# Narrowing the moving operand of a mixture's matmuls from 256 to 224 columns, and splitting a queue of twelve scatters into pairs

## The chip, the cores and the metric

The kernel runs on one core of a Trainium2 chip. The metric is the device time of one execution in microseconds (us); the kernel before takes 814.52 us, the median of three runs (814.19 to 816.84).

## The reference, cut to what matters

Three layers follow one another on 1536 tokens of 512 features. A retention layer makes the tokens. The first mixture sends each token to the one of eight experts that its gate prefers; each expert takes at most `capacity` = 384 tokens, in token order. The second mixture runs all tokens through four experts and adds them up, weighted by `domain_probs`.

```python
expert_idx = np.argmax(x @ w_gate, axis=1)
...
for i in range(N):                      # N = 1536, E = 8, capacity = N // E * 2 = 384
    e = expert_idx[i]
    if counts[e] < capacity:
        disp[e, counts[e]] = x[i]; pos[i] = counts[e]; counts[e] += 1; keep[i] = True
h = np.maximum(np.einsum('ecd,edf->ecf', disp, w1), 0.0)    # D = 512 -> F = 1024
y = np.einsum('ecf,efd->ecd', h, w2)
...
for e in range(4):                      # second mixture, all tokens
    out += p[:, e:e + 1] * (np.maximum(x @ w1[e], 0.0) @ w2[e])
```

With the reference's default inputs the gate gives the eight experts 183, 196, 188, 167, 213, 180, 203 and 206 tokens.

## The kernel before

The work runs in stages, one behind another on TensorE (PE). The order of every engine is that of the code; tile pools and semaphores add the waits.

Retention and routing come first (up to 91 us). Each of 12 blocks of 128 tokens is computed, written to a table in DRAM (`xd`), and its gate, its expert and its rank within the expert are worked out. From these come `gidx` (for each expert and each of `SL` = 256 slots the row of `xd` that sits there; an empty slot points at a row of zeros), `offi` (the column at which an expert's tokens begin in the sorted order) and `nbi` (whether any expert has more tokens than slots). If one has, the branch in `overflow()` (L566 to L654) runs the surplus in blocks of 128; otherwise it is jumped over.

The first mixture is the loop over `e` (L785 to L830). Numbers are split into a high part rounded to the matmul type fp32r and a rest, and each product is three fp32r matmuls (`PASS`). An expert has 8 weight chunks of 512 KB, which SP loads into `raw` tiles (4 buffers), ACT copies to the high part (L105) and DVE subtracts to the rest (L106), six chunks ahead (`split_w`, `DEPTH`). Per expert:

- m1 (L795): 4 groups of 24 matmuls, 128x128 weights, 256 moving columns (`x[:, sx, k]`, the slots). Two halves (`ff`) share one PSUM bank of 512 columns. Each group is evacuated by ACT (relu, L779) and DVE (rest, L780) over 512 columns.
- `prep_x(e + 1)` (L669): 8 transposes turn the next expert's gathered rows around, ACT and DVE copy them (L683, L684), and POOL gathers the rows of expert `e + 3` (L556, two indirect DMAs).
- for `e` = 0 `tables()` (L717): DVE and ACT compute for each token its four output weights (`tt`) and its place in the sorted order (`posi`). POOL then issues 12 scatters (L768) that write `tt` to the DRAM table `td`, one behind another since all write the same tile, and reads the table back as `tl` (L772). `tl` is first used by the second mixture's evacuations (L873).
- m2 (L817): 2 groups of 48 matmuls with 256 moving columns, each evacuated to the sorted columns `ds(ra, SL)` of `x2h` (ACT, L825) and `x2l` (DVE, L826). An expert's unused slots lie over the next expert's columns and are overwritten by it.

The second mixture (L836 to L891) does the same with 512 moving columns: n1 (L846) and n2 (L867), 24 stages of 96 matmuls. The tail scatters the rows to the output.

Where the trace names an F32 matmul (L297, L307, L338, L488) one call of the program is two instructions; an fp32r matmul (L795, L817, L846, L867) is one.

Of the kernel before, what the change touches and what calls it, by code (L numbers as in the profile page):

```python
# [8 lines left out]
F32 = mybir.dt.float32  # L9
# [10 lines left out]
P = 128  # L20
# [7 lines left out]
KF = F // P  # L28
XW = KD * 136
SL = 256  # L30
FMAX = 3.4028234663852886e38
PASS = ((0, 0), (0, 1), (1, 0))
WARM0 = 11
# [9 lines left out]


def blocks_of(cap):
    return max(SL // P, -(-min(cap, N) // P))


@with_exitstack
def tile_retention_moe_moe(ctx: ExitStack, tc, qkv, cst, gqt, a1, a2, b1, b2, dp, out, cap):  # L50
    nc = tc.nc
    NB = blocks_of(cap)
    drops = cap < N
    general = NB > SL // P

    pc = ctx.enter_context(tc.tile_pool(name="pc", bufs=1))
    pd = ctx.enter_context(tc.tile_pool(name="pd", bufs=1, space=DRAM))
# [82 lines left out]
    with ExitStack() as actx:  # L140
# [378 lines left out]
        nc.vector.tensor_tensor(out=cnt[:, 1], in0=cps, in1=cnt[:, 0], op=ALU.subtract)  # L519
        if general:  # L520
            nc.vector.tensor_scalar(
                out=nbf, in0=cnt[:, 0], scalar1=float(SL), scalar2=None, op0=ALU.is_gt
            )
            for j in range(3, NB):
                nc.vector.scalar_tensor_tensor(
                    out=nbf, in0=cnt[:, 0], scalar=float(j * P), in1=nbf,
                    op0=ALU.is_gt, op1=ALU.add,
                )
            nc.vector.tensor_copy(nbi[:, 0:8], nbf)
            nc.vector.tensor_reduce(out=nbi[:, 8:9], in_=nbf, axis=AX.X, op=ALU.max)  # L530
# [35 lines left out]
    def overflow():  # L566
        some = nc.values_load(nbi[0:1, 8:9], min_val=0, max_val=NB)
        with tc.If(some > 0), tc.tile_pool(name="pg", bufs=1, side="right") as pg:
            clear_x2()
            nx = NB - SL // P  # L570
            gi = pg.tile([P, nx, E1], I32, name="gi")
            rkm = pg.tile([P, NT], F32, name="rkm")
            nc.vector.tensor_scalar(
# [5 lines left out]
            for i in range(NT):  # L579
                for b in range(nx):  # L580
                    at = pg.tile([P, P], F16, tag="gat", name=f"gat{i}_{b}")
                    nc.vector.tensor_scalar(
                        out=at, in0=rnk[:, 0:P], scalar1=float(SL + b * P),
                        scalar2=rkm[:, i:i + 1], op0=ALU.add, op1=ALU.is_equal,
                    )
                    nc.tensor.matmul(
                        out=bk[:, b * E1:(b + 1) * E1], lhsT=at, rhs=ohk[:, i],
                        start=(i == 0 and b == 0), stop=(i == NT - 1), skip_group_check=True,
                    )
            nc.vector.tensor_copy(gi.rearrange("p b e -> p (b e)"), bk[:, 0:nx * E1])  # L590
            with tc.For_i(0, E1, 1) as e:
                blocks = nc.values_load(nbi[0:1, ds(e, 1)], min_val=0, max_val=NB - 2)
                col0 = nc.values_load(
                    offi[0:1, ds(e, 1)], engines=(ET.Activation, ET.DVE), min_val=0, max_val=N
                )
                w1 = pg.tile([P, 4, KD, 256], F32, name="gw1")
                w2 = pg.tile([P, 4, KF, P], F32, name="gw2")
                nc.sync.dma_start(
                    out=w1.rearrange("p c k f -> p c (k f)"),
                    in_=a1[ds(e, 1)].rearrange("o c p x -> p (o c) x"),  # L600
                )
                nc.sync.dma_start(
                    out=w2.rearrange("p c k f -> p c (k f)"),
                    in_=a2[ds(e, 1)].rearrange("o c p x -> p (o c) x"),
                )
                with tc.For_i(0, blocks, 1) as j:
                    xg = pe.tile([P, D], F32, tag="xe", name="gx")
                    xh = pe.tile([P, KD + KF, P], F32, tag="xet", name="gxh")
                    gc = pg.tile([P, 1], I32, name="gc")
                    nc.vector.tensor_copy(  # L610
                        gc, gi.rearrange("p b e -> p (b e)")[:, ds(j * E1 + e, 1)]
                    )
                    nc.gpsimd.indirect_dma_start(
                        out=xg, out_offset=None, in_=xd,
                        in_offset=bass.IndirectOffsetOnAxis(ap=gc, axis=0),
                    )
                    bk = bank("gt")
                    for k in range(KD):
                        nc.tensor.transpose(
                            bk[:, k * P:(k + 1) * P], xg[:, k * P:(k + 1) * P], ident  # L620
                        )
                    nc.vector.tensor_copy(xh[:, 0:KD].rearrange("p a t -> p (a t)"), bk)
                    for q in range(2):
                        bk = bank("g1")
                        for r in range(4):
                            f = 4 * q + r
                            for k in range(KD):
                                nc.tensor.matmul(
                                    out=bk[:, r * P:(r + 1) * P],
                                    lhsT=w1[:, f // 2, k, (f % 2) * P:(f % 2 + 1) * P],  # L630
                                    rhs=xh[:, k], start=(k == 0), stop=(k == KD - 1),
                                )
                        nc.scalar.activation(
                            out=xh[:, KD + 4 * q:KD + 4 * q + 4].rearrange("p a t -> p (a t)"),
                            in_=bk, func=AF.Relu,
                        )
                    bk = bank("g2")
                    for d in range(KD):
                        for k in range(KF):
                            nc.tensor.matmul(  # L640
                                out=bk[:, d * P:(d + 1) * P], lhsT=w2[:, d, k], rhs=xh[:, KD + k],
                                start=(k == 0), stop=(k == KF - 1),
                            )
                    b3 = bk.rearrange("p (a t) -> p a t", a=KD)
                    col = nc.s_assert_within(
                        col0 + j * P + SL, 0, N + SL - P,
                        skip_runtime_bounds_check_because="a block that runs starts before the "
                        "last kept token, and those are at most N",
                    )
# [7 lines left out]
    xet[0] = pw.tile([P, 2, 1024], F32R, tag="w", name="xet0").rearrange(  # L657
        "p s (k t) -> p s k t", k=KD
    )
    if drops and cap < SL:  # L660
        clear_x2()
    if general:
        overflow()
# [53 lines left out]
    def tables():  # L717
# [46 lines left out]
            )  # L764
            nc.vector.tensor_tensor(out=tmpb, in0=tmpb, in1=tmpc, op=ALU.add)
        nc.vector.tensor_tensor(out=posi, in0=tmpb, in1=ranks, op=ALU.add)
        for i in range(NT):
            nc.gpsimd.indirect_dma_start(  # L768
                out=td, out_offset=bass.IndirectOffsetOnAxis(ap=posi[:, i:i + 1], axis=0),
                in_=tt[:, i], in_offset=None,  # L770
            )
        nc.gpsimd.dma_start(out=tl, in_=td.rearrange("(i p) c -> p i c", p=P))  # L772

    def h_tile(name):
        return ph.tile([P, 512], F32R, tag="h", name=name)

    def evac_h(bk, name):
        hh, hl = h_tile(name + "h"), h_tile(name + "l")
        nc.scalar.activation(out=hh, in_=bk, func=AF.Relu)  # L779
        nc.vector.scalar_tensor_tensor(  # L780
            out=hl, in0=bk, scalar=0.0, in1=hh.bitcast(F32), op0=ALU.max, op1=ALU.subtract
        )
        return hh, hl

    for e in range(E1):  # L785
        x = xet.pop(e)
        hs = []
        for c in range(4):
# [3 lines left out]
            for ff in range(2):  # L792
                for n, (sx, sw) in enumerate(PASS):
                    for k in range(KD):
                        nc.tensor.matmul(  # L795
                            out=bk[:, ff * SL:(ff + 1) * SL],
                            lhsT=w[:, sw, k, ff * P:(ff + 1) * P], rhs=x[:, sx, k],
                            start=(k == 0 and n == 0), stop=(k == KD - 1 and n == 2),
                        )
            hs.append(evac_h(bk, f"h{e}_{c}"))  # L800
            del ws[u]
            split_w(u + DEPTH)
        if e + 1 < E1:
            prep_x(e + 1)
        if e == 0:
            tables()
        ra = nc.scalar.value_load(offi[0:1, e:e + 1], min_val=0, max_val=N)
        rv = nc.vector.value_load(offi[0:1, e:e + 1], min_val=0, max_val=N)
        for g in range(2):
            bk = bank(f"m2_{e}_{g}")  # L810
            for q in range(2):
                u = 8 * e + 4 + 2 * g + q
                w = ws[u].rearrange("p s (k d) -> p s k d", k=KF)
                for k in range(KF):
                    hcols = slice((k % 2) * SL, (k % 2 + 1) * SL)
                    for n, (sw, sh) in enumerate(PASS):
                        nc.tensor.matmul(  # L817
                            out=bk[:, q * SL:(q + 1) * SL], lhsT=w[:, sw, k],
                            rhs=hs[k // 2][sh][:, hcols],
                            start=(k == 0 and n == 0), stop=(k == KF - 1 and n == 2),  # L820
                        )
                del ws[u]
                if q == 1:
                    b3 = bk.rearrange("p (a t) -> p a t", a=2)
                    nc.scalar.copy(x2h[:, 2 * g:2 * g + 2, ds(ra, SL)], b3)  # L825
                    nc.vector.tensor_tensor(  # L826
                        out=x2l[:, 2 * g:2 * g + 2, ds(rv, SL)], in0=b3,
                        in1=x2h[:, 2 * g:2 * g + 2, ds(rv, SL)].bitcast(F32), op=ALU.subtract,
                    )
                split_w(u + DEPTH)  # L830
    mctx.close()
# [62 lines left out]
def consts(cap):  # L894
# [23 lines left out]
    c[:, C_U:C_TIE] = (s < t)  # L918
    c[:, C_TIE:C_TOK] = 8.0 - np.arange(8)[None, :]
    c[:, C_TOK:C_RNK] = 1 + s + P * np.arange(NT)[None, :]  # L920
    c[:, C_RNK:] = np.where(np.arange(SL) < cap, np.arange(SL), -1)[None, :]
    return c, gq[1:].astype(np.float32).reshape(NCH - 1, P, 512)


# [59 lines left out]
```

## Time and profile before

| What | us |
|---|---|
| Median of three runs | 814.52 |
| Profiled execution | 812.81 |
| Its span, first to last instruction | 811.0 |
| Retention and routing, 0 to 91.35 | 91.35 |
| First mixture, 91.35 to 282.34 | 190.99 |
| Second mixture and tail, 282.34 to 811.0 | 528.7 |
| Busy in the span: PE matmuls | 791.4 (98%) |
| Busy in the span: PE weight loads (PEld) | 691.3 (85%) |
| Busy in the span: DVE, ACT, POOL | 340.4, 227.7, 91.1 |

PE is matmul time, PEld the loading of the stationary 128x128 operand, which goes on beside the matmuls. The ends of matmuls are modelled and their records overlap, so the time of one matmul in a row is read from how many start in a stretch and not from its own duration. A line such as `0.97 ... x8` in a timeline is a group of eight merged instructions that took 0.97 us from the first start to the last end.

### The profile page before, as it was taken

The page shows a single profiled execution, that of the slowest core. Times are in us where ns is not written, and L with a number is a line of the kernel's source. Part 1 is how long each engine was busy: PE and PEld are TensorE (multiplying, and loading weights), DVE is VectorE, ACT ScalarE, POOL GpSimd, SP SyncE. Part 2 cuts the span into 40 slices and gives each one's busy share as a digit, 9 for nine tenths or more (in the row PEclk, how much of TensorE's full clock was granted, in tenths as well). Part 3 has the DMA queues.
Part 4 walks back from the last instruction along what each step waited for, and adds up shares of the span by engine and source line. Part 5 has one row for each costly group of instructions (what it writes and reads, how often), then busy time and mean ns, then how long its engine had stood idle before and what let it go on. Part 6 is the DMA issues. An engine that isn't in the chain of part 4 may idle for free.

```text
span 811.0 us, 11249 instructions
## 1 busy us (share of the span) xinstructions
PE 791.4 (98%) x4700; PEld 691.3 (85%) x4701; DVE 340.4 (42%) x549; ACT 227.7 (28%) x351; POOL 91.1 (11%) x81
## 2 busy tenths in 40 slices
PE   8988999999999999999999999999999999999997
PEld 5877899999999988888888888888888888888886
DVE  7999786656666541212252121234121225121221
ACT  4555455555455430101231010303020123011010
POOL 6563322231000000000000000000000000000101
PEclk9999999999999999999999999999999999999998
DMA  9784576685655630000141000024000011000101
GB/s 324 270 280 144 189 245 204 163 260 185 201 169 176 199 83 1 0 1 1 31 133 45 0 1 1 1 90 119 1 0 1 1 52 53 20 33 13 40 1 52
DMA packets 24872, 76.64 MB, mean 94 GB/s; under 512 B 4945, under 2 KB 5217, under 8 KB 24818
## 3 DMA queue, kind: packets, MB, share of 16 engines
q1 hardware_dynamic: 20016, 68.21, 26.5%
q0 software_dynamic: 2672, 7.44, 2.7%
q8 instruction: 38, 0.62, 0.3%
q10 hardware_dynamic: 2130, 0.23, 0.2%
q14 instruction: 16, 0.13, 0.1%
HBM read 69.53 MB, written 6.34 MB: 94 GB/s over the span
## 4 chain that ended last, share of the span: by engine, by line
PE 88%; DVE 7%; DMA 1%; ACT 1%; issue 1%; POOL 0%; POOLq 0%; ACTq 0%
PE n L846 32%; PE n L867 32%; PE m L795 11%; PE m L817 11%; DVE qpad L215 4%; DVE sd L263 1%; PE T L677 1%; DMA xe<-xd,gidx 1%; DVE w L106 1%; DMA qk<-qkv 1%; PE S L257 1%; DVE lgs L352 0%; ACT st L287 0%; ACT qpad L214 0%; DMA out_dram<-acc,tl 0%
## 5 line engine op out<-in xcount | busy, mean ns | idle before, releaser
L846 PE MATMUL n<-x2h,w 128*128 128x512 f32 x768 | 238.4, 389 | 0.0
L846 PEld LDWEIGHTS n<-x2h,w 128*128 128x128 f32 x768 | 144.2, 188 | 29.8
L846 PE MATMUL n<-x2l,w 128*128 128x512 f32 x384 | 149.4, 389 | 0.0
L106 DVE TENSOR_TENSOR w<-raw,w 128x1024 fp32r<-128x1024 f32 x96 | 118.3, 1243 | 17.2 <-ACT w L105 17.1
L105 ACT CAST w<-raw 128x1024 fp32r<-128x1024 f32 x96 | 98.3, 1046 | 4.0 <-DMA raw<-a 3.5
L795 PE MATMUL m<-xet,w 128*128 128x256 f32 x768 | 93.7, 283 | 0.8 <-DVE xet L697 0.5
L795 PEld LDWEIGHTS m<-xet,w 128*128 128x128 f32 x768 | 92.8, 192 | 1.0 <-ACT xet L697 0.7
L878 DVE SCALAR_TENSOR_TENSOR acc<-n,tl,acc 128x512 f32<-128x512 f32 (+1 forms) x37 | 27.2, 736 | 156.7 <-PE n L867 156.7
L846 PEld LDWEIGHTS n<-x2l,w 128*128 128x128 f32 x384 | 72.1, 188 | 15.1 <-DVE x2l L826 0.2
L883 POOL DMA_INDIRECT out_dram<-acc,tl x12 | 11.6, 966 | 592.4 <-DVE acc L878 592.4
L779 ACT ACTIVATE g_0h<-n 128x512 fp32r<-128x512 f32 x12 | 7.2, 598 | 252.6 <-PE n L846 252.6
L215 DVE TENSOR_TENSOR qpad<-qk,qpad 64x512 fp32r<-64x512 f32 x24 | 31.6, 1316 | 2.3 <-ACT qpad L214 1.9
L257 PE MATMUL S<-qpad,ks 128*128 128x256 f32 x144 | 23.9, 305 | 8.7 <-DVE qpad L215 8.0
L873 DVE TENSOR_SCALAR acc<-n,tl 128x512 f32<-128x512 f32 x12 | 9.0, 751 | 51.2 <-PE n L867 51.2
L257 PEld LDWEIGHTS S<-qpad,ks 128*128 128x128 f32 x144 | 19.2, 195 | 13.2 <-DVE qpad L215 10.0
L867 PE MATMUL n<-w,g_1h 128*128 128x512 f32 (+1 forms) x98 | 29.7, 385 | 0.0
L867 PE MATMUL n<-w,g_2h 128*128 128x512 f32 (+1 forms) x98 | 29.7, 385 | 0.0
L867 PE MATMUL n<-w,g_3h 128*128 128x512 f32 (+1 forms) x98 | 29.7, 385 | 0.0
L867 PE MATMUL n<-w,g_4h 128*128 128x512 f32 (+1 forms) x98 | 29.7, 385 | 0.0
L867 PE MATMUL n<-w,g_5h 128*128 128x512 f32 (+1 forms) x98 | 29.7, 385 | 0.0
L867 PE MATMUL n<-w,g_6h 128*128 128x512 f32 (+1 forms) x98 | 29.7, 385 | 0.0
L867 PE MATMUL n<-w,g_7h 128*128 128x512 f32 (+1 forms) x98 | 29.7, 385 | 0.0
(185 smaller groups left out, 1234.7 us busy)
## 6 DMA issues: line engine op xcount, KB each, us to landing
raw<-a SPq DMA_DIRECT2D x64, 512.0 KB, 3.6
raw<-b SPq DMA_DIRECT2D x32, 512.0 KB, 3.6
qk<-qkv SPq DMA_DIRECT2D x12, 512.0 KB, 6.6
kv<-qkv SPq DMA_DIRECT2D x12, 512.0 KB
xd<-xk SPq DMA_DIRECT2D x12, 256.0 KB, 2.8
gqs<-gqt SPq DMA_DIRECT2D x5, 256.0 KB, 6.1
cdec<-cst SPq DMA_DIRECT2D x1, 536.0 KB, 5.9
iw<-cst SPq DMA_DIRECT2D x1, 272.0 KB
```

The lines of the kernel that those rows point to most:

```text
L105: nc.scalar.copy(w[:, 0], r)
L106: nc.vector.tensor_tensor(out=w[:, 1], in0=r, in1=w[:, 0].bitcast(F32), op=ALU.subtract)
L215: nc.vector.tensor_tensor(out=qp[r, 1, :, j], in0=qT[r], in1=qp[r, 0, :, j].bitcast(F32), op=ALU.subtract,)
L257: nc.tensor.matmul(out=bks[hp // 2][:, (hp % 2) * SL:(hp % 2 + 1) * SL], lhsT=ks[:, a, hp], rhs=qp[:, b, hp], start=(n == 0 and hp % 2 == ...
L263: nc.vector.tensor_tensor(out=sd[:, g], in0=bks[g], in1=dec[:, g], op=ALU.mult)
L795: nc.tensor.matmul(out=bk[:, ff * SL:(ff + 1) * SL], lhsT=w[:, sw, k, ff * P:(ff + 1) * P], rhs=x[:, sx, k], start=(k == 0 and n == 0), st ...
L817: nc.tensor.matmul(out=bk[:, q * SL:(q + 1) * SL], lhsT=w[:, sw, k], rhs=hs[k // 2][sh][:, hcols], start=(k == 0 and n == 0), stop=(k == K ...
L846: nc.tensor.matmul(out=bk, lhsT=w[:, sw, k, ff * P:(ff + 1) * P], rhs=x2[sx][:, k, g * 512:(g + 1) * 512], start=(k == 0 and n == 0), stop ...
L867: nc.tensor.matmul(out=bk[:, 0:width], lhsT=hs[k][sh][:, t * P:(t + 1) * P], rhs=w[:, sw, k % 2, cols], start=(k == 0 and n == 0), stop=(k ...
L873: nc.vector.tensor_scalar(out=acc[i][:, cols], in0=bk[:, 0:width], scalar1=sc, scalar2=None, op0=ALU.mult,)
L878: nc.vector.scalar_tensor_tensor(out=acc[i][:, cols], in0=bk[:, 0:width], scalar=sc, in1=acc[i][:, cols], op0=ALU.mult, op1=ALU.add,)
L883: nc.gpsimd.indirect_dma_start(out=out, out_offset=bass.IndirectOffsetOnAxis(ap=tl[:, i, 4:5].bitcast(I32), axis=0), in_=acc[i], in_offset ...
```

## The change

The moving operand of m1 and m2 shrinks from 256 to `SM` = 224 columns. Tiles keep their 256-column pitch, so that each operand starts where it did. The evacuations follow: two runs of 224 columns in place of 512. `rnk` has no slot beyond 223, so that those 32 slots point at the row of zeros; gathers and transposes keep their 256 slots. The branch for surplus tokens begins at 224 in place of 256, its code has two blocks in place of one, and `nbi` takes one more small DVE instruction. The twelve scatters leave `tables()` and are issued two per expert for `e` = 0 to 5, behind that expert's gathers; the read of `tl` follows the last.

```diff
+SM = 224
...
 def blocks_of(cap):
-    return max(SL // P, -(-min(cap, N) // P))
+    return max(0, -(-(min(cap, N) - SM) // P))
...
             nc.vector.tensor_scalar(
-                out=nbf, in0=cnt[:, 0], scalar1=float(SL), scalar2=None, op0=ALU.is_gt
-            )
-            for j in range(3, NB):
+                out=nbf, in0=cnt[:, 0], scalar1=float(SM), scalar2=None, op0=ALU.is_gt
+            )
+            for j in range(1, NB):
                 nc.vector.scalar_tensor_tensor(
...
+    def scatter(some):
+        for i in some:
             nc.gpsimd.indirect_dma_start(
                 out=td, out_offset=bass.IndirectOffsetOnAxis(ap=posi[:, i:i + 1], axis=0),
                 in_=tt[:, i], in_offset=None,
             )
-        nc.gpsimd.dma_start(out=tl, in_=td.rearrange("(i p) c -> p i c", p=P))
+        if NT - 1 in some:
+            nc.gpsimd.dma_start(out=tl, in_=td.rearrange("(i p) c -> p i c", p=P))
...
-    def evac_h(bk, name):
+    def evac_h(bk, name, slots=False):
         hh, hl = h_tile(name + "h"), h_tile(name + "l")
-        nc.scalar.activation(out=hh, in_=bk, func=AF.Relu)
+
+        def used(a):
+            return a.rearrange("p (a t) -> p a t", a=2)[:, :, 0:SM] if slots else a
+
+        nc.scalar.activation(out=used(hh), in_=used(bk), func=AF.Relu)
...
                         nc.tensor.matmul(
-                            out=bk[:, ff * SL:(ff + 1) * SL],
-                            lhsT=w[:, sw, k, ff * P:(ff + 1) * P], rhs=x[:, sx, k],
+                            out=bk[:, ff * SL:ff * SL + SM],
+                            lhsT=w[:, sw, k, ff * P:(ff + 1) * P], rhs=x[:, sx, k, 0:SM],
...
+        if e < E1 - 2:
+            scatter(range(2 * e, 2 * e + 2))
...
-                    hcols = slice((k % 2) * SL, (k % 2 + 1) * SL)
+                    hcols = slice((k % 2) * SL, (k % 2) * SL + SM)
...
-                            out=bk[:, q * SL:(q + 1) * SL], lhsT=w[:, sw, k],
+                            out=bk[:, q * SL:q * SL + SM], lhsT=w[:, sw, k],
...
-                    nc.scalar.copy(x2h[:, 2 * g:2 * g + 2, ds(ra, SL)], b3)
+                    nc.scalar.copy(x2h[:, 2 * g:2 * g + 2, ds(ra, SM)], b3)
```

On PE, at the beginning of the first mixture, expert 0's four m1 groups (`m_0_0` to `m_0_3`, output; `xet`, moving; `w`, weights) and the first transposes stand so before:

```order
L795 MATMUL m_0_0_1490<-xet_1252,w_820 128x256 x24
L795 MATMUL m_0_1_1524<-xet_1252,w_908 128x256 x24
L795 MATMUL m_0_2_1558<-xet_1252,w_1470 128x256 x24
L795 MATMUL m_0_3_1592<-xet_1252,w_1475 128x256 x24
L677 MATMUL T_0_1627<-ident,xe_1458 128x128 x2
```

And so in the changed kernel:

```order
L804 MATMUL m_0_0_1527<-xet_1253,w_820 128x224 x24
L804 MATMUL m_0_1_1561<-xet_1253,w_908 128x224 x24
L804 MATMUL m_0_2_1595<-xet_1253,w_1507 128x224 x24
L804 MATMUL m_0_3_1629<-xet_1253,w_1512 128x224 x24
L678 MATMUL T_0_1664<-ident,xe_1495 128x128 x2
```

The number of matmuls and their order stay; each of them has 32 moving columns less, and the transposes keep their 128.

On POOL, from the gather of expert 3 (`xe_1641`) on, the queue before is this (`xe_1971`, `xe_2265`, `xe_2559` and `xe_2853` are the gathers of experts 4 to 7):

```order
L556 DMA xe_1641<-xd,gidx 128x512 x2
L742 IOTA tt 128x12
L768 DMA td<-tt,posi 1536x8 x12
L772 DMA tl<-td 128x12x8
L556 DMA xe_1971<-xd,gidx 128x512 x2
L556 DMA xe_2265<-xd,gidx 128x512 x2
L556 DMA xe_2559<-xd,gidx 128x512 x2
L556 DMA xe_2853<-xd,gidx 128x512 x2
```

In the changed kernel the same stretch is:

```order
L557 DMA xe_1678<-xd,gidx 128x512 x2
L743 IOTA tt 128x12
L771 DMA td<-tt,posi 1536x8 x2
L557 DMA xe_1997<-xd,gidx 128x512 x2
L771 DMA td<-tt,posi 1536x8 x2
L557 DMA xe_2293<-xd,gidx 128x512 x2
L771 DMA td<-tt,posi 1536x8 x2
L557 DMA xe_2589<-xd,gidx 128x512 x2
L771 DMA td<-tt,posi 1536x8 x2
L557 DMA xe_2885<-xd,gidx 128x512 x2
L771 DMA td<-tt,posi 1536x8 x4
L776 DMA tl<-td 128x12x8
```

The gather of expert 4 stood behind twelve scatters and the read of `tl`, and stands behind two scatters now; the read of `tl` has moved behind the last gather.

## Rows read from the trace of the kernel before

**Rows 1.** The page's chain that ended last: shares by engine, then by line.

```profile
PE 88%; DVE 7%; DMA 1%; ACT 1%; issue 1%; POOL 0%; POOLq 0%; ACTq 0%
PE n L846 32%; PE n L867 32%; PE m L795 11%; PE m L817 11%; DVE qpad L215 4%; DVE sd L263 1%; PE T L677 1%; DMA xe<-xd,gidx 1%; DVE w L106 1%; DMA qk<-qkv 1%; PE S L257 1%; DVE lgs L352 0%; ACT st L287 0%; ACT qpad L214 0%; DMA out_dram<-acc,tl 0%
```

**Rows 2.** The chain in order of time, from the first mixture: start us, us, what.

```profile
103.52 0.87 PE T L677 x8
104.39 11.51 PE m L817 x96
115.90 11.52 PE m L795 x96
...
175.22 0.87 PE T L677 x8
...
282.34 21.85 PE n L846 x96
304.18 21.76 PE n L867 x96
```

**Rows 3.** Busy time in two windows: one expert, then one stage of the second mixture.

```profile
core 0: us, PE busy (x) PEld busy (x) DVE busy (x) ACT busy (x) POOL busy (x), PEclk, DMA share, GB/s
...
187.60:211.50 23.90, 23.90 (x202) 23.90 (x202) 14.97 (x16) 12.07 (x16) 2.19 (x2) 1.00 0.62 200
...
347.70:369.46 21.76, 21.76 (x98) 18.02 (x97) 2.94 (x4) 0.60 (x1) 0.00 (x0) 1.00 0.00 1
```

**Rows 4.** Timeline of weight loads where m1 begins, PE idle before: start us, us, instruction.

```profile
91.32 0.19 PEld L795 LDWEIGHTS m<-xet,w 128*128 128x128 f32 x1 [0.67 <-ACT xet L697]
...
91.43 0.31 PEld L795 LDWEIGHTS m<-xet,w 128*128 128x128 f32 x2
```

**Rows 5.** Timeline of weight loads for F32 matmuls of 128, 136 and 128 columns.

```profile
78.91 0.97 PEld L297 LDWEIGHTS O<-qg,st 128*128 128x128 f32 x8
79.87 0.99 PEld L338 LDWEIGHTS X<-iw,xT 128*128 128x128 f32 x8
...
81.02 0.85 PEld L307 LDWEIGHTS O<-sd,kv 128*64 128x64 f32 x16
```

**Rows 6.** Groups by line: weight loads of 128 and of 64 columns, mean ns last.

```profile
L795 PEld LDWEIGHTS m<-xet,w 128*128 128x128 f32 x768 | 92.8, 192 | 1.0 <-ACT xet L697 0.7 <-issue 0.4
...
L307 PEld LDWEIGHTS O<-sd,kv 128*64 128x64 f32 x192 | 10.7, 141 | 1.1
```

**Rows 7.** Waits from 104 to 283 us: us in total, times, longest us.

```profile
ACT x2h L825 <- PE m L817: 48.5, 15, 3.3
...
POOL td L768 <- DMA td<-tt,posi: 30.8, 11, 4.0
...
ACT h_3h L779 <- PE m L795: 9.7, 8, 1.3
```

**Rows 8.** POOL's timeline: first scatter, read of `tl`, gather of expert 4.

```profile
113.05 1.95 POOL L768 DMA_INDIRECT td<-tt,posi  x1 [2.63 <-DVE posi L766]
...
160.76 1.07 POOL L772 DMA_DIRECT2D tl<-td  x1 [3.31 <-DMA td<-tt,posi]
162.14 1.01 POOL L556 DMA_INDIRECT xe<-xd,gidx  x1 [0.30 <-issue]
163.46 0.95 POOL L556 DMA_INDIRECT xe<-xd,gidx  x1 [0.30 <-issue]
```

**Rows 9.** DMA issues: size, median us from issue to landing.

```profile
raw<-a SPq DMA_DIRECT2D x64, 512.0 KB, 3.6
...
xe<-xd,gidx POOLq DMA_INDIRECT x16, 4.8
```

**Rows 10.** ACT's timeline at the end of expert 0's m1.

```profile
102.18 1.05 ACT L105 CAST w<-raw 128x1024 fp32r<-128x1024 f32 x1 [0.30 <-DMA raw<-a]
103.55 0.60 ACT L779 ACTIVATE h_3h<-m 128x512 fp32r<-128x512 f32 x1 [0.33 <-PE m L795]
```

**Rows 11.** DVE's timeline: the count instruction, and the copies after the branch.

```profile
86.76 0.16 DVE L521 TENSOR_SCALAR nbf<-cnt 128x8 f32<-128x8 f32 x1
...
89.99 0.69 DVE L701 TENSOR_TENSOR xet<-T0u,xet 128x512 fp32r<-128x512 f32 x1 [1.29 <-DVEq L568]
90.88 0.42 DVE L697 CAST xet<-T0x 128x256 fp32r<-128x256 f32 x1 [0.20 <-PE T0x L497]
```

More of the change, by code (lines that the diff above doesn't have):

```diff
@@ L53, in tile_retention_moe_moe @@
     drops = cap < N
-    general = NB > SL // P
+    general = NB > 0
     pc = ctx.enter_context(tc.tile_pool(name="pc", bufs=1))
@@ L521, in tile_retention_moe_moe @@
             nc.vector.tensor_scalar(
-                out=nbf, in0=cnt[:, 0], scalar1=float(SL), scalar2=None, op0=ALU.is_gt
+                out=nbf, in0=cnt[:, 0], scalar1=float(SM), scalar2=None, op0=ALU.is_gt
             )
-            for j in range(3, NB):
+            for j in range(1, NB):
                 nc.vector.scalar_tensor_tensor(
-                    out=nbf, in0=cnt[:, 0], scalar=float(j * P), in1=nbf,
+                    out=nbf, in0=cnt[:, 0], scalar=float(SM + j * P), in1=nbf,
                     op0=ALU.is_gt, op1=ALU.add,
@@ L569, in overflow @@
             clear_x2()
-            nx = NB - SL // P
+            nx = NB
             gi = pg.tile([P, nx, E1], I32, name="gi")
@@ L582, in overflow @@
                     nc.vector.tensor_scalar(
-                        out=at, in0=rnk[:, 0:P], scalar1=float(SL + b * P),
+                        out=at, in0=rnk[:, 0:P], scalar1=float(SM + b * P),
                         scalar2=rkm[:, i:i + 1], op0=ALU.add, op1=ALU.is_equal,
@@ L591, in overflow @@
             with tc.For_i(0, E1, 1) as e:
-                blocks = nc.values_load(nbi[0:1, ds(e, 1)], min_val=0, max_val=NB - 2)
+                blocks = nc.values_load(nbi[0:1, ds(e, 1)], min_val=0, max_val=NB)
                 col0 = nc.values_load(
@@ L645, in overflow @@
                     col = nc.s_assert_within(
-                        col0 + j * P + SL, 0, N + SL - P,
+                        col0 + j * P + SM, 0, N + SL - P,
                         skip_runtime_bounds_check_because="a block that runs starts before the "
@@ L659, in tile_retention_moe_moe @@
     )
-    if drops and cap < SL:
+    if drops and cap < SM:
         clear_x2()
@@ L766, in tables @@
         nc.vector.tensor_tensor(out=posi, in0=tmpb, in1=ranks, op=ALU.add)
-        for i in range(NT):
+    def scatter(some):
+        for i in some:
             nc.gpsimd.indirect_dma_start(
@@ L771, in tables @@
             )
-        nc.gpsimd.dma_start(out=tl, in_=td.rearrange("(i p) c -> p i c", p=P))
+        if NT - 1 in some:
+            nc.gpsimd.dma_start(out=tl, in_=td.rearrange("(i p) c -> p i c", p=P))
     def h_tile(name):
         return ph.tile([P, 512], F32R, tag="h", name=name)
-    def evac_h(bk, name):
+    def evac_h(bk, name, slots=False):
         hh, hl = h_tile(name + "h"), h_tile(name + "l")
-        nc.scalar.activation(out=hh, in_=bk, func=AF.Relu)
+        def used(a):
+            return a.rearrange("p (a t) -> p a t", a=2)[:, :, 0:SM] if slots else a
+        nc.scalar.activation(out=used(hh), in_=used(bk), func=AF.Relu)
         nc.vector.scalar_tensor_tensor(
-            out=hl, in0=bk, scalar=0.0, in1=hh.bitcast(F32), op0=ALU.max, op1=ALU.subtract
+            out=used(hl), in0=used(bk), scalar=0.0, in1=used(hh.bitcast(F32)),
+            op0=ALU.max, op1=ALU.subtract,
         )
@@ L795, in tile_retention_moe_moe @@
                         nc.tensor.matmul(
-                            out=bk[:, ff * SL:(ff + 1) * SL],
-                            lhsT=w[:, sw, k, ff * P:(ff + 1) * P], rhs=x[:, sx, k],
+                            out=bk[:, ff * SL:ff * SL + SM],
+                            lhsT=w[:, sw, k, ff * P:(ff + 1) * P], rhs=x[:, sx, k, 0:SM],
                             start=(k == 0 and n == 0), stop=(k == KD - 1 and n == 2),
                         )
-            hs.append(evac_h(bk, f"h{e}_{c}"))
+            hs.append(evac_h(bk, f"h{e}_{c}", True))
             del ws[u]
@@ L823, in tile_retention_moe_moe @@
                 if q == 1:
-                    b3 = bk.rearrange("p (a t) -> p a t", a=2)
-                    nc.scalar.copy(x2h[:, 2 * g:2 * g + 2, ds(ra, SL)], b3)
+                    b3 = bk.rearrange("p (a t) -> p a t", a=2)[:, :, 0:SM]
+                    nc.scalar.copy(x2h[:, 2 * g:2 * g + 2, ds(ra, SM)], b3)
                     nc.vector.tensor_tensor(
-                        out=x2l[:, 2 * g:2 * g + 2, ds(rv, SL)], in0=b3,
-                        in1=x2h[:, 2 * g:2 * g + 2, ds(rv, SL)].bitcast(F32), op=ALU.subtract,
+                        out=x2l[:, 2 * g:2 * g + 2, ds(rv, SM)], in0=b3,
+                        in1=x2h[:, 2 * g:2 * g + 2, ds(rv, SM)].bitcast(F32), op=ALU.subtract,
                     )
@@ L920, in consts @@
     c[:, C_TOK:C_RNK] = 1 + s + P * np.arange(NT)[None, :]
-    c[:, C_RNK:] = np.where(np.arange(SL) < cap, np.arange(SL), -1)[None, :]
+    c[:, C_RNK:] = np.where(np.arange(SL) < min(cap, SM), np.arange(SL), -1)[None, :]
     return c, gq[1:].astype(np.float32).reshape(NCH - 1, P, 512)
```

## The prediction

> **What bounds the kernel now.** I read the chain that ended last first. PE has 88% of it [rows 1]; the two mixtures alone, L795, L817, L846 and L867, make 86%. In order of time the chain is, from 103.52 us on, one PE stage directly behind another: 96 matmuls of m2 in 11.51 us, 96 of m1 in 11.52, a block of 8 transposes in 0.87 [rows 2]. No other engine appears between them, so whatever shortens a matmul of the first mixture shortens the span, as long as nobody else becomes late.
>
> The windows by expert say who could. In one expert's 23.90 us PE is busy throughout, DVE 14.97, ACT 12.07, at a granted clock of 1.00, the 2.4 GHz level [rows 3]. The waits agree: ACT waits for PE before a relu (up to 1.3 us each) and before a copy to `x2h` (up to 3.3 us each) [rows 7]; the evacuating engines stand idle for PE.
>
> **What a matmul costs.** A stage of 96 takes 11.515 us with 256 columns (120.0 ns each) and 21.76 with 512 (226.7 ns each) [rows 2]. The difference is 106.7 ns for 256 columns, 0.417 ns a column, and the rest, 13.3 ns, is there at either width. If that line goes on to 224 columns, a matmul takes 120.0 - 32 x 0.417 = 106.6 ns.
>
> **What may stop it.** Each matmul needs a 128x128 weight load of its own. Its record lasts 192 ns [rows 6], but loads overlap: the next begins before the one ahead has ended. How close can they follow? Where m1 begins PE had been idle, and the first load of an fp32r matmul starts at 91.32, the second at 91.43, the third 0.31 - 0.19 = 0.12 later [rows 4]. The first two have no streaming matmul ahead of them, so 0.11 us may be the load's own pace. The F32 rows bound it from both sides. Eight loads of 128 columns take 0.97 us, so (0.97 - 0.19) / 7 = 111 ns from start to start; their matmuls have only 128 columns and the load can't need more than that. Sixteen loads of 64 columns take 0.85 us: (0.85 - 0.14) / 15 = 47 ns, so 95 for 128 [rows 5]. The records' lengths, 192 against 141 ns for 64 columns more [rows 6], give 102. So the load needs between 95 and 111 ns, and a matmul of 224 columns takes between 106.6 ns (load hidden) and 111 ns (load bound). I take the middle, 108.8: 0.11 is the row nearest to this case, but it is rounded to 10 ns. The rows with 64-column loads also show that PE takes a load and a matmul every 47 ns, so their issue is no limit.
>
> The Trainium skill (TensorE: Matmul & The Clock Gate, LDWEIGHTS (loading the stationary operand)) gives a load as its columns over 1.2 per ns; for 128 columns that is an estimate of 106.7 ns, and with it the load would just hide behind 224 columns. No row here decides between 106.7 and 111; by the page the first term below would be 20.5 us and not 17.1.
>
> **The change, part by part.**
>
> *Matmuls.* 8 experts x (96 + 96) = 1536 matmuls go from 120.0 to 108.8 ns: 1536 x 11.15 ns = **-17.1 us** (between -20.5 at 106.6 and -13.8 at 111). The 56 transposes keep their columns: 0.
>
> *Evacuations.* 448 in place of 512 columns for ACT and DVE. They can only get shorter, and PE doesn't wait for them now: 0. An expert's period falls to about 23.9 - 192 x 11.15 ns = 21.8 us; DVE's 15.0 and ACT's 12.1 us fit into that [rows 3], and the weight chunks, 8 x 512 KB at 3.6 us from issue to landing, have six chunks of lead [rows 9]. Without this cover each late chunk would cost what is missing.
>
> *Expert 0.* Its beginning is the one place where ACT works without slack: it waits for a chunk until 102.18, copies it for 1.05 us, and comes to the last relu at 103.55 [rows 10]. PE would reach m2 at about 104.39 - 96 x 11.15 ns = 103.3, and needs that relu and DVE's rest only 18 matmuls (2.0 us) later, at 105.3. The relu can't start before about 103.25, behind the copy; relu and rest take 0.6 and 0.7 us, and DVE has a split of 1.2 us before it. That ends about 105.2. It may fit or miss: **+0.2 us** (0 to 0.6).
>
> *Surplus count.* One more DVE instruction of about 0.16 us in the chain that feeds the branch. Behind the branch DVE's copy at 89.99 took 0.69, and the next one at 90.88 waited 0.20 us for PE, which waits for the gather [rows 11]. That 0.20 covers it, though not by much: I take **+0.1** (0 to 0.2). The longer branch body is jumped over: 0.
>
> *Scatters.* Twelve instructions before and after; what changes is the queue. Before, they run from 113.05 to the read of `tl` at 160.76, 30.8 us of it waiting for each other, and the gather of expert 4 comes behind them at 162.14 and 163.46 [rows 7, 8]. With 4.8 us to landing [rows 9] it is there at 168.3; its transposes begin at 175.22 [rows 2]: 6.9 us of slack. In the narrower kernel these transposes come seven stages earlier by 7 x 96 x 11.15 ns = 7.5 us, so with the old queue PE would have waited 0.6 us (2.1 at 106.6 ns). With the pairs the gather of expert 4 stands behind two scatters, which are over before the transposes of expert 2 release its buffer. So this part is worth **0** in the sum, and is what keeps the first term whole. Behind each pair on POOL stands the next gather, which isn't released until a period later; a pair takes at most two issues of 2 us and two waits of 4 us [rows 7, 8]. The last four scatters follow the gather of expert 7, which the transposes at 175.22 + 23.9 = 199.1, less 9.6 now, release: at 6 us each they bring `tl` to about 215 to 220 us. Its first reader is in the second mixture's n2, behind 304.18 - 17 = 287 [rows 2]. Without that cover of some 65 us a late `tl` would stop the accumulations.
>
> *Second mixture.* Not touched: 0.
>
> Sum: -17.1 + 0.2 + 0.1 = -16.8. The profiled execution took 812.81 us, so 796.0; the median of the runs lies 1.7 above it, and by that the forecast is **797.7 us**. At the ends of the load's pace it is 794.3 and 801.1.
>
> **The rivals.**
>
> *Weight-bound already: no change.* 120.0 ns at 256 columns might be the load's pace and not the stream's. For it speaks that PEld is busy 23.90 of 23.90 us in the first mixture, against 18.02 of 21.76 in the second [rows 3]. The Trainium skill (Perfetto Trace Analysis, Identifying the Most-Contended Engine) judges TensorE's headroom by this share and not by the matmuls' busy time; by that rule the first mixture has no headroom in its columns, and the time would stay at 814.5. Against it: the loads here overlap each other, so that their busy time can't tell how much of it is needed; the F32 loads followed each other in 111 ns [rows 5], and the 13.3 ns that 256 columns take beyond their stream are there with 512 too, where loads leave (21.76 - 18.02) / 97 = 39 ns free per matmul [rows 3]. The time: 814.5, within 0.3%. Chance 0.09.
>
> *In between, or another pace-setter.* Either the 13.3 ns come on top of a load of 100 to 107 ns (113 to 119 ns a matmul, 1.5 to 10.8 us saved), or an engine or queue that the faster stages catch up with gives part back. For the first speaks that nothing shows fp32r loads at less than 111; against the second the slack above. 803 to 812 us. Chance 0.11.
>
> *Slower: fp32r doesn't keep its pace below 256 columns.* Every fp32r matmul of the trace has 256 or 512. The only ones below 256 are F32, in two instructions each: 136 columns take (0.99 - 0.19) / 7 = 114 ns per instruction, 128 take 111 [rows 5], about 0.83 ns a column. If a 224-column fp32r matmul fell to that form, it would cost 2 x (111 + 96 x 0.83) = 381 ns, 1536 x 261 ns = +401 us, about 1215. It decides from small amounts on: 2.4 us, 0.3%, are reached at 121.6 ns a matmul. Nothing in the trace speaks for it, and the straight line from 512 to 256 speaks against a step; but no row lies below. Chance 0.08.
>
> *The surplus branch runs.* It would if an expert had over 224 tokens; the default inputs give 213 at most. It reads every expert's 4 MB again, 34 MB, at the 200 GB/s of [rows 3] 168 us and so above 960. Chance 0.02.
>
> **How the numbers follow.** The forecast holds 0.68, its own range 794 to 801.5; 0.11 lie between, 0.09 at no change, 0.10 slower, and 0.02 below 794. For 8 in 10 the range takes in the forecast's and the case between: 793 to 811. 0.3% of 814.5 us, 2.4 us, is about what the measurement can tell from no change. Faster: 0.68 + 0.02 + 0.10 of the case between = 0.80. Same: 0.09 + 0.01 = 0.10. Slower: 0.10.
>
> **What would show it.** In the chain of the changed kernel m1 and m2 stages of 96 take 10.2 to 10.7 us in place of 11.5, with the transposes still at 0.87 and no other engine between; a stage at 11.5 shows the first rival, at 36 the third. The second mixture's stages stay at 21.76. Fp32r loads start 107 to 111 ns apart. ACT's waits for PE before a relu are shorter, but are there. The gather of expert 4 is issued at about 125 us, and `tl` lands before 230. If PE waits for ACT, DVE or a DMA inside the first mixture after expert 0, the sum is wrong in its covers; if it doesn't and the stages are not in this range, it is wrong in the matmul's price.

## The result, and the profile after

The changed kernel takes 802.27 us, the median of four runs (801.25 to 803.14), against 814.41 before: a ratio of 0.984 (95% interval 0.982 to 0.987). It is faster by 12.1 us, inside the stated range and 4.6 us short of the forecast. The profiled execution took 802.98 us, 9.8 less than that of before; the terms below are worked out from these two, and the other 2.3 us of the 12.1 lie between the profiled executions and the medians.

The chain that ended last, in order of time (start us, us, what), answers to [rows 2]:

```profile
91.22 0.79 PE m L804 x5
92.01 1.68 issue
93.69 11.95 PE m L804 x91
105.64 0.87 PE T L678 x8
106.52 10.71 PE m L828 x96
117.23 10.72 PE m L804 x96
...
172.57 0.87 PE T L678 x8
...
272.53 21.85 PE n L857 x96
294.38 21.76 PE n L878 x96
```

Two things are to be seen. A stage of 96 matmuls takes 10.715 us in place of 11.515, so 111.6 ns a matmul in place of 120.0. And the first stage is not like the others: after five matmuls PE stands still for 1.68 us in which it "waited for nothing that the profile shows", and the other 91 take 11.95 us where 91 x 111.6 ns would be 10.16. The same place before, which the prediction did not look at, is this:

```profile
91.35 2.27 PE m L795 x17
93.89 9.62 PE m L795 x79
```

There the pause came after 17 matmuls and lasted 0.27 us (93.89 - 93.62).

The windows around the pause (busy us and count of PE, PEld, DVE, ACT, POOL, then the granted clock, the DMA share and GB/s), and below them one expert, which answers to [rows 3]:

```profile
core 0: us, PE busy (x) PEld busy (x) DVE busy (x) ACT busy (x) POOL busy (x), PEclk, DMA share, GB/s
92.00:93.70 1.70, 0.02 (x2) 0.00 (x1) 1.70 (x2) 1.70 (x3) 1.39 (x2) 1.00 0.27 41
93.70:95.00 1.30, 1.30 (x9) 1.30 (x9) 1.30 (x2) 0.95 (x2) 1.00 (x2) 0.69 0.85 265
95.00:97.00 2.00, 2.00 (x11) 2.00 (x11) 1.47 (x2) 0.00 (x0) 1.70 (x2) 0.50 0.80 297
97.00:98.00 1.00, 1.00 (x9) 1.00 (x7) 0.00 (x0) 0.37 (x1) 0.40 (x1) 0.70 0.75 283
98.00:100.00 2.00, 2.00 (x20) 2.00 (x19) 1.48 (x2) 1.11 (x2) 0.00 (x0) 1.00 0.99 352
195.75:218.07 22.32, 22.32 (x203) 22.32 (x202) 14.68 (x17) 11.75 (x17) 8.12 (x7) 1.00 0.69 215
```

Behind the pause the granted clock fell to 0.50, the 1.2 GHz level, from about 94.2 to 97.6 us: the records of 11 matmuls fall into 2 us there, 20 at full clock. Before, the clock stayed at 1.00 behind the short pause. From the next stage on PE is busy without a gap in every expert's 22.32 us.

The balance of the two profiled executions: 16 stages x 0.80 = -12.8; the pause +1.4 (1.68 against 0.27); the half clock +1.65 (1.79 lost in the 91 matmuls, 0.14 in the 79 of before); m1's start -0.13. That is -9.9, and the second mixture begins at 272.53 in place of 282.34, 9.8 us earlier. From there on nothing moved: 528.7 us are left in both.

Four weight loads in a row in m2, which answer to [rows 4], follow each other in 0.11 us:

```profile
195.82 0.19 PEld L828 LDWEIGHTS m<-h_0h,w 128*128 128x128 f32 x1
195.93 0.19 PEld L828 LDWEIGHTS m<-h_0l,w 128*128 128x128 f32 x1
196.04 0.19 PEld L828 LDWEIGHTS m<-h_0h,w 128*128 128x128 f32 x1
196.15 0.19 PEld L828 LDWEIGHTS m<-h_1h,w 128*128 128x128 f32 x1
```

And POOL's timeline at the places of [rows 8]: gather of expert 4, last scatter, read of `tl`:

```profile
129.10 0.98 POOL L557 DMA_INDIRECT xe<-xd,gidx  x1 [7.74 <-PE T L678]
...
210.70 0.96 POOL L771 DMA_INDIRECT td<-tt,posi  x1 [1.82 <-DMA td<-tt,posi]
213.32 1.07 POOL L776 DMA_DIRECT2D tl<-td  x1 [1.67 <-DMA td<-tt,posi]
```

The gather of expert 4 is issued 33 us earlier than before and 43 us ahead of its transposes at 172.57; `tl` is read 59 us before the second mixture begins.

### The profile page after: what moved, and what is told of

The parts are those of the page before. It is cut to its first block, busy times and chain, and to the rows that moved or that the text cites. A ratio compares the mean times of both kernels' runs of the same rounds, so it can differ in the third digit from the quotient of the medians.

```text
span 801.2 us, 11248 instructions
## 1 busy us (share of the span) xinstructions
PE 779.7 (97%) x4700; PEld 678.9 (85%) x4701; DVE 338.7 (42%) x550; ACT 224.7 (28%) x351; POOL 93.4 (12%) x81
## 4 chain that ended last, share of the span: by engine, by line
PE 87%; issue 1%; DMA 0%; POOLq 0%; DVE 0%
PE n L857 33%; PE n L878 32%; PE m L804 11%; PE m L828 11%; PE T L678 1%; DMA out_dram<-acc,tl 0%; POOLq L991 0%; DVE acc L889 0%; POOLq L894 0%
## 5 line engine op out<-in xcount | busy, mean ns | idle before, releaser
L804 PE MATMUL m<-xet,w 128*128 128x224 f32 x768 | 88.9, 277 | 2.1 <-issue 1.7
L804 PEld LDWEIGHTS m<-xet,w 128*128 128x128 f32 x768 | 88.1, 195 | 2.4 <-issue 1.8
```

Of the source, the lines that this page charges most:

```text
L804: nc.tensor.matmul(out=bk[:, ff * SL:ff * SL + SM], lhsT=w[:, sw, k, ff * P:(ff + 1) * P], rhs=x[:, sx, k, 0:SM], start=(k == 0 and n == 0 ...
```

## The experiments

Two questions were open: what holds a matmul at 111.6 ns, and where the pause and the half clock come from.

**Fewer columns still.** In m1 the second and third product stream 128 columns; the corrections that they add are left out for the slots from 128 on.

```diff
-                            out=bk[:, ff * SL:ff * SL + SM],
-                            lhsT=w[:, sw, k, ff * P:(ff + 1) * P], rhs=x[:, sx, k, 0:SM],
+                            out=bk[:, ff * SL:ff * SL + (P if n else SM)],
+                            lhsT=w[:, sw, k, ff * P:(ff + 1) * P],
+                            rhs=x[:, sx, k, 0:P if n else SM],
```

> The changed kernel, but the second and third of m1's three products stream 128 columns, not 224 (so their small corrections are left out for the slots from 128 on); m2 stays. If a matmul can't follow the one before it sooner than its weight load, the starts stay 111.6 ns apart, an m1 stage of 96 stays at 10.7 us and the time at about 802. If the 111.6 ns are the stream's with a larger fixed part (18.3 ns and 0.417 a column), a 128-column matmul takes 72 ns, the stage 8.2 us, and the time falls by 20 us to 782. If fp32r loses its pace below some width, a 128-column matmul takes 222 ns like F32, the stage 17.8 us, and the time rises to about 858.

Its chain:

```profile
94.08 18.09 PE m L804 x91
112.17 1.73 PE T L678 x8
113.90 11.82 PE m L829 x96
125.73 10.68 PE m L804 x96
```

And three of its windows, with the columns of the windows above:

```profile
96.00:112.00 16.00, 16.00 (x77) 16.00 (x77) 6.00 (x7) 4.55 (x6) 1.07 (x2) 0.50 0.66 237
...
115.00:120.00 5.00, 5.00 (x42) 5.00 (x42) 4.27 (x20) 1.34 (x2) 1.88 (x3) 0.89 0.68 213
126.00:136.00 10.00, 10.00 (x92) 10.00 (x91) 6.90 (x8) 5.68 (x8) 0.97 (x1) 1.00 0.73 237
```

The steady m1 stage takes 10.68 us although two thirds of its matmuls have 96 columns less than the others: 111.3 ns each. So it is not the stream that sets the pace, and fp32r at 128 columns does not fall to F32's 222 ns, which would have shown as 17.8 us. That it is the weight load and not a fixed price of each matmul follows with [rows 5]: with loads of 64 columns PE took a load and a matmul of 128 columns (F32) every 47 ns. The whole run, a single one, took 811.36 us and not 802, for another reason: the first m1 stage was at half clock from 95.6 us to its end, and the clock came back only in m2 with its 224 columns. Against full clock that is 18.09 - 10.1 in this stage, 0.9 in the transposes and 1.1 in m2, 10.0 us in all; the changed kernel had lost 1.8 of this kind itself, and the pause here is 0.5 us longer.

Three weight loads in a row of that m2, at half clock:

```profile
114.34 0.33 PEld L829 LDWEIGHTS m<-h_0l,w 128*128 128x128 f32 x1
114.55 0.33 PEld L829 LDWEIGHTS m<-h_0h,w 128*128 128x128 f32 x1
114.77 0.33 PEld L829 LDWEIGHTS m<-h_1h,w 128*128 128x128 f32 x1
```

They follow each other in 0.21 to 0.22 us, and so do the m1 loads of that stretch (213 ns by their starts in the trace), against 0.11 at full clock: the pace of the loads goes with TensorE's clock.

**Widths between 224 and 256.** `SM` = 240, 248 and 252, nothing else.

```diff
-SM = 224
+SM = 240
```

> The changed kernel with 240 columns in place of 224. If a matmul takes the longer of the straight line (13.3 ns and 0.417 a column) and the load's 111.6 ns, it takes 113.3 ns, a stage of 96 takes 10.88 us, and the time is 2.6 us above the changed kernel's. If 256 columns were bound by the load and 224 have some other price, the stage lies elsewhere: at 11.1 us on the line through 10.72 and 11.52.

> The changed kernel with 248 columns, for the stages of 96 alone. On the straight line through 256 and 512 columns a matmul takes 116.7 ns and a stage 11.20 us. With 240 columns a stage took 10.75 and not the 10.88 of that line. If the fixed part of 13.3 ns is smaller below 256, a stage takes less than 11.1 us; if the load is all that counts below 256, 10.75.

> The changed kernel with 252 columns, for the stages of 96 alone. On the straight line a matmul takes 118.3 ns and a stage 11.36 us; with a smaller fixed part below 256, less than 11.2; if the load is all that counts below 256, 10.75.

The same m1 or m2 stage of the three chains, 240 columns first, then 248 and 252:

```profile
138.03 10.76 PE m L804 x96
```

```profile
139.17 11.04 PE m L804 x96
```

```profile
139.60 11.20 PE m L804 x96
```

That is 112.0, 115.0 and 116.6 ns a matmul. At 0.417 ns a column, 248 and 252 have a fixed part of 11.7 ns, where 256 and 512 had 13.3. So the straight line of the prediction was good only down to 256: at 240 it gave a stage of 10.88 us, and 10.75 came. But two of the fifteen full-clock stages at 248 columns are shorter than the others:

```profile
184.92 10.88 PE m L804 x96
```

That is 113.3 ns, a fixed part of 10.0, at the same width. So 11.7 is not a constant, and how a matmul's time is made up just above the load's pace stays open. What the rows show is where the load takes over: 240 columns cost PE 0.4 ns a matmul more than 224, 248 columns 1.7 to 3.4 more. The times, 801.86, 806.14 and 808.80 us, are of one execution each; that 240 columns come out no slower than 224, where 2.6 us more were expected, is no saving of the width, as that execution had no half clock behind its pause (1.62 us).

**The jump.** The pause stands right behind the surplus branch, whose code the change made longer: 24 more PE instructions (12 loads and 12 matmuls) that are jumped over. Theory: the pause is the fetch of the instructions behind the jump, and how many matmuls come before it depends on how far the jump lands from the end of what is already there. Rival: it belongs to the narrower matmuls or to another edit. Three kernels change the number of blocks in the branch's code and, of what runs, nothing but the small DVE instructions of the surplus count (one less or one more). The first leaves out the surplus above 352 tokens of an expert.

One block:

```diff
-    return max(0, -(-(min(cap, N) - SM) // P))
+    return min(1, max(0, -(-(min(cap, N) - SM) // P)))
```

Three blocks:

```diff
-    return max(0, -(-(min(cap, N) - SM) // P))
+    return 1 + max(0, -(-(min(cap, N) - SM) // P))
```

The kernel before, with two blocks in place of one:

```diff
-    return max(SL // P, -(-min(cap, N) // P))
+    return 1 + max(SL // P, -(-min(cap, N) // P))
```

> The changed kernel with one block in place of two in the code of the surplus branch, which is jumped over; the jump is as long as in the kernel before (tokens above 352 in one expert are left out, there are none). If the pause of 1.7 us after the fifth matmul of m1 is the fetch of the code behind the jump, it comes after the seventeenth again, as before, and is 0.5 to 0.7 us long, and the half clock behind it does not come: 799 to 801. If the pause belongs to the narrower matmuls or the other edits, it stays after the fifth at 1.7 us, and the time at 802.

> The changed kernel with three blocks in the code of the surplus branch, a jump as much longer again as the change made it. If the pause is where a fetched piece of code ends, the jump now lands behind that end, the next one is far off, and there is no pause in the first matmuls of m1, nor the half clock: 798 to 800. If the length of the jump is what costs, the pause grows above 1.7 us: 803 or more. If neither, it stays at 802.

> The kernel before, 256 columns and scatters unsplit, with one block more in the code of the surplus branch, as the change has it. If the fetch behind the jump makes the pause, it comes after the fifth matmul here too and is 1.6 to 1.9 us long, with the half clock behind it in some runs: 815.5 to 818. If the pause belongs to the other edits, nothing changes: 814.4.

The chain with one block:

```profile
91.14 2.13 PE m L804 x17
93.27 0.64 issue
93.91 8.97 PE m L804 x79
```

PE's timeline with three blocks:

```profile
94.39 4.00 PE L804 MATMUL m<-xet,w 128*128 128x224 f32 x21 [3.62 <-DVE w L107]
```

And POOL's:

```profile
94.31 1.84 POOL L557 DMA_INDIRECT xe<-xd,gidx  x1 [0.43 <-PEq L569]
```

The chain of the kernel before with two blocks:

```profile
92.28 0.83 PE m L795 x5
93.11 1.51 issue
94.62 11.07 PE m L795 x91
```

With one block the pause is back behind the 17th matmul, 0.64 us long, and the half clock is gone: 800.19 us (ratio to the kernel before 0.982, 0.978 to 0.985), 2.1 us less than the changed kernel. The kernel before took 813.36 us beside this one and 814.41 beside the changed kernel, so the profiles decide: expert 0's m1, with its pause, takes 11.75 us here and 14.42 in the changed kernel, 2.67 less, and the later stages take the same. With three blocks there is no matmul before the pause at all, PE begins m1 at 94.39, and half clock follows: 804.52 us (0.987, 0.984 to 0.990). (The DVE split that the row names as releaser is of a later chunk; m1's first chunk was split in the retention stage. POOL's row, which waits until 94.31 for PE's own sequencer at the branch, PEq L569, says the same: PE had not got to these instructions.) My expectation of a landing behind the end, without a pause, was wrong. In the kernel before, with its 256 columns, two blocks move the pause behind the fifth matmul: the rival is out. There the time, 815.43 us against 813.36 on the same chip (1.001, 0.998 to 1.003), says nothing by itself, and the profiled execution kept the full clock.

The number of matmuls before the pause falls from 17 to 5 and to 0 with 24 PE instructions more each time (a matmul here is a load and a matmul, so 12 of them are 24 instructions). When PE goes on can be read from the DMA view, whose queue q8 carries PE's instructions: in the second mixture it moves one packet of 16 KB every 29.0 us, and in that time PE runs 128 matmuls and 128 loads. In the changed kernel one such packet starts at 91.24 us and has landed at 92.27. It is the only packet of any queue from 91.2 to 92.3 us:

```profile
q8 instruction: 1, 0.02, 5.8%
```

| Kernel | matmuls before the pause | packet on q8 landed, us | PE goes on, us |
|---|---|---|---|
| before | 17 | 92.46 | 93.89 |
| before, two blocks | 5 | 93.27 | 94.62 |
| changed, one block | 17 | 92.57 | 93.91 |
| changed | 5 | 92.27 | 93.69 |
| changed, three blocks | 0 | 92.40 | 94.39 |

In all twelve profiles such a packet starts between 91.0 and 92.3 us, and PE goes on 1.3 to 1.6 us after it has landed (2.0 with three blocks). So the pause ends a fixed while behind the packet, and how long it is depends on how many instructions PE still had. That it is a wait for the code behind the jump is shown as far as the order of these events can show it; what happens in the 1.3 to 1.6 us after the landing has no row and stays open.

The half clock is another matter. With 224 columns it came behind each of the three long pauses that were profiled (changed, unsplit, three blocks) and behind neither of the two of 0.6 us, but a long pause does not bring it by itself. The chain with 248 columns:

```profile
91.86 1.82 issue
93.68 10.62 PE m L804 x91
```

That pause is longer than the changed kernel's, and the 91 matmuls behind it run at 116.7 ns each, at a granted clock of 1.00 up to the end of the stage. So removing the block removed both pause and half clock here, but why the clock fell after 1.68 us and not after 1.82 is open.

**Both blocks, fewer instructions.** This version keeps the surplus branch for every capacity, but merges its slot matmuls: both blocks are moving columns of one matmul per token block.

```diff
-                    nc.tensor.matmul(
-                        out=bk[:, b * E1:(b + 1) * E1], lhsT=at, rhs=ohk[:, i],
+                nc.tensor.matmul(
+                    out=bk[0:E1, 0:nx * P], lhsT=ohk[:, i], rhs=at,
...
+            for b in range(nx):
+                nc.tensor.transpose(
+                    bk[:, b * E1:(b + 1) * E1], gt[:, b * P:(b + 1) * P], ident[0:E1, 0:E1]
+                )
```

> The changed kernel with both blocks kept in the surplus branch, but its slot matmuls merged: the two blocks are 256 moving columns of one matmul per token block, and two transposes turn the result around, 26 PE instructions or a few more in place of 48. The branch is jumped over as ever. If the end of the fetched code makes the pause, it comes after 15 or 16 matmuls and is about 0.7 to 1.0 us, without the half clock: 800 to 801. If what helped with one block was something other than the number of PE instructions jumped over, it stays at 802.

Its chain:

```profile
91.31 1.90 PE m L811 x15
93.22 0.61 issue
93.82 9.20 PE m L811 x81
```

Two matmuls earlier than with one block, as the two transposes more in the code ask for. It takes 800.38 us (0.983, 0.979 to 0.986), the same as with one block, and has the lowest time of the versions that keep both blocks. The branch itself did not run here, as no expert has surplus tokens.

**The scatters, each way.** The kernel before with the scatters in pairs, and the changed kernel with all twelve for expert 0:

```diff
         if e == 0:
             tables()
+        if e < E1 - 2:
+            scatter(range(2 * e, 2 * e + 2))
```

```diff
-        if e < E1 - 2:
-            scatter(range(2 * e, 2 * e + 2))
+        if e == 0:
+            scatter(range(NT))
```

> The kernel before, 256 columns, with the scatters issued two per expert as the change has them, and nothing else of it. If that part is worth nothing by itself, the time is that of the kernel before, 813 to 814.5, and PE's stages stay at 11.52 us. If scatters beside the gathers of every expert make a late gather or slow the weight chunks, a stage of the first mixture is longer and the time above 815.5.

> The changed kernel with all twelve scatters issued for expert 0, as before. By the prediction's working the gather of expert 4 comes behind them; m1 began 3 us late in the changed kernel's profile and the period is 22.3 us, so it should land 2 to 3 us ahead of its transposes: no wait, 802. If the scatters go on longer than the 48 us of before, PE waits for that gather: 803 to 806, with a DMA ahead of the transposes of expert 4 in the chain.

By themselves the pairs change nothing that can be measured: 813.07 against 814.17 us (0.998, 0.995 to 1.000), stages at 11.52. Unsplit, the changed kernel takes 809.89 us (805.54 to 813.48; ratio to the kernel before 0.994, 0.991 to 0.997, where the pairs have 0.984, 0.982 to 0.987), 7.6 more than with pairs. POOL's timeline there:

```profile
116.23 1.96 POOL L771 DMA_INDIRECT td<-tt,posi  x1 [2.62 <-DVE posi L767]
...
172.49 1.07 POOL L776 DMA_DIRECT2D tl<-td  x1 [1.49 <-DMA td<-tt,posi]
173.87 1.01 POOL L557 DMA_INDIRECT xe<-xd,gidx  x1 [0.31 <-PE m L804]
```

And its chain at the transposes of expert 4:

```profile
173.87 5.03 DMA xe<-xd,gidx
178.89 0.14 issue
179.03 1.94 PE T L678 x8
180.97 12.80 PE m L828 x96
```

The twelve scatters took 56 us from the first to the read of `tl`, not the 48 of before, so that the gather was issued only when PE already wanted its rows. (The row names a matmul as the gather's releaser; its 0.31 us is the usual gap between POOL's instructions, and the gather simply came behind the read of `tl`.) PE waited 5.2 us, and then the transposes and m2 lost 3.2 us more at half clock (0.74 in the window from 180 to 190 us), 8.3 in all. In the profiled executions the second mixture begins 9.6 us later than with pairs; the rest, 1.3, is mostly the first m1 stage, whose pause and half clock were longer this time. Both my figures, no wait and 803 to 806, were too low.

## Why the prediction was right, and where its terms were off

**Bound.** Right: PE's stages stand one behind another before and after, and the time fell by what they lost, 12.8 us, less what expert 0's first stage took longer.

**The matmul's price.** The mechanism was right, load against stream, and the size was off. "I take the middle, 108.8" between 106.6 and 111 is the step that failed: the load binds at 111.6, the upper end, which the F32 loads of [rows 5] had given. 1536 x 8.33 ns = 12.8 us in place of 17.1. The experiment with 128 columns shows that no stream is involved at that pace. The Trainium skill (TensorE: Matmul & The Clock Gate, LDWEIGHTS (loading the stationary operand)) leads to an estimate of 106.7 ns for 128 columns. The runs show 111.3 to 111.6 from one load to the next, and these decide. The prediction's straight line does not hold below 256 either (115.0 ns at 248 columns, not 116.7), but at 224 the load hides that.

**Weight-bound already.** Wrong as a forecast for 256 columns, where the stream and not the load set the 120 ns. The Trainium skill (Perfetto Trace Analysis, Identifying the Most-Contended Engine) names the busy share of the weight loads as one of two measures of TensorE's headroom. That share was 100% of an expert's time before and is 100% after (22.32 of 22.32 us), while the time of a matmul fell by 7%. With loads that overlap each other it cannot tell the two cases apart. What could was their distance.

**fp32r below 256 columns.** No slower pace came at 252, 248, 240, 224 or 128 columns: the third rival is out. What the stream alone takes at 224 is hidden by the load.

**Expert 0.** The forecast was +0.2 us from ACT; it lost 3.1 us more than before in the profile, and not by ACT, which waited for PE (1.2 us) before each of the last three relus.

**"The longer branch body is jumped over: 0"** is the step that was wrong in kind. The branch costs nothing to skip, but PE's code behind it comes later: 1.4 us of pause and 1.65 of half clock in the profile. Taking the block out again gave 2.67 us in the profile and 2.1 in the timed runs. For the profiled execution the forecast was 796.0 and it took 802.98: of these 7.0 us the load's price makes 4.3, the pause 1.4 and the half clock 1.65, less the 0.3 that the forecast had for expert 0 and the count and 0.13 of m1's earlier start. The medians miss by less, 4.6, and that is luck: the prediction carried over the 1.7 us by which the median of before lay above its profiled execution, and after the change the median lies 0.7 below. Two of the four runs, with a mean clock of 0.998 and 0.999 over the execution, are 1.4 to 1.9 us faster than the two with 0.993 and 0.995. Whether they went without the half clock in m1 is not shown: the profiled execution of before has a mean of 0.993 too, and none of its half clock lies in m1 (a part is the stretch from 62.8 to 66.2 us, at 0.50).

**Scatters.** Right to value them at 0 in the sum and as the cover of the first term; the price of the missing cover, 0.6 to 2.1 us, was far too small: 8.3 in the profile, 7.6 in the medians. The prediction took the 48 us that the twelve had needed, and had no term for what a stopped PE loses after it goes on.

**The rest.** As forecast: transposes 0.87, second mixture 21.76, the gather of expert 4 issued at 129 us (forecast 125), `tl` read at 213 us, ACT's waits for PE shorter and still there, no wait for ACT, DVE or a DMA after expert 0.

## What to carry to other kernels

A matmul with its own weight load costs about the longer of stream and load, and the load's pace is read from the distance of starts where the stream is short, not from busy shares or from the length of a record; once a row gives that distance, take it and not a middle. Narrowing pays down to the width where the two meet, here about 240 columns, and nothing below. Code that is jumped over is not free where the engine is the bound: look at what stands right behind the jump, and keep the skipped body short. And price a stop of TensorE with what may follow it at half clock: a gather that came 5.2 us late cost 8.3.

## What the runs showed of the hardware that was not expected

- With 224 columns the granted clock fell to 0.50 for about 3.4 us after a pause of 1.68 us and for 6.8 us around one of 1.83 (scatters unsplit); after pauses of 0.61 and 0.64 us it did not fall. After 1.62, 1.82 and 1.66 us with 240, 248 and 252 columns and 1.51 us with 256 it stayed at 1.00 in m1. So the length of the pause alone does not decide, and what does is open.
- With two thirds of the matmuls at 128 columns the clock stayed at 0.50 for the rest of that stage, over 16 us, though PE was busy throughout; later stages of the same form ran at 1.00, having come to it from m2.
- The distance of weight loads is 111 ns at full clock and 213 at half.
- Behind the skipped branch PE goes on 1.3 to 1.6 us after the next 16 KB packet of its instructions has landed (2.0 in one kernel).
- The fixed part of an fp32r matmul is 13.3 ns at 256 and 512 columns, 11.7 at 252, and at 248 it is 11.7 in most stages and 10.0 in two. Why is open.
